# Spreading gate tiles over a recurrence: four tiles per three chunks instead of four per four

## The chip, the cores and the metric

The kernel runs on one core of a Trainium2 chip. The metric is the device time of one execution in microseconds (us), median of several. A fast run has a granted TensorE clock of 0.97 to 0.99 over the whole run. Ratios are the mean time of one kernel's fast runs over that of the kernel before in the same rounds on the same chip, so they are not quite the ratio of the medians quoted beside them. The studies ran on several chips; the kernel before has a median of 509.9 us on the first and 508.4 to 508.6 us, with a spread of 506.6 to 510.8, on the others.

## The reference

```python
# q, k, v, alpha: (4, 8, 768, 48)
for t in range(S):                      # gated linear attention
    state = alpha[:, :, t, :, None] * state + einsum('bhd,bhe->bhde', k[:, :, t], v[:, :, t])
    y[:, :, t] = einsum('bhd,bhde->bhe', q[:, :, t], state)
x = y as (3072 tokens, 384)
out = ((x @ w1) * (x @ w2)) @ w3 @ w_out      # w1, w2: 384x1024; w3: 1024x1024; w_out: 1024x384
```

The recurrence is computed in chunks of 128 tokens, 24 in all (six per batch row). Every three chunks give a group of 384 tokens; a group's gate product `(x@w1)*(x@w2)` is made in eight tiles of 128 columns. `w3 @ w_out` is folded once and multiplied last. The weights come as 64-bit floats and are converted on the chip.

## The kernel before

TensorE is shared by two kinds of work: attention, chunk after chunk, and gate tiles. A gate tile is a generator with two *pieces* of nine matmuls each; `run(k)` issues k pieces from a queue, at three places in a chunk.

```python
def split_x(g, i):                  # x of a group becomes three exact parts
    x = st.pop(("xT", g))
    t = tr[i].tile([C, 3, KM, TG], FP32R, tag="x3", name="x3")    # one buffer
    nc.scalar.activation(t[:, 0], x, AF.Copy, scale=1.0 - 2.0 ** -13)           # L369
    nc.vector.tensor_sub(t[:, 1], x, t[:, 0].bitcast(FP32))                     # L370
    nc.vector.scalar_tensor_tensor(t[:, 2], ...)                                # L371

def exact(to, w, x, scale):         # one piece
    # six matmuls with parts 0 and 1 (L380), evacuation on ScalarE (L382),
    # three matmuls with part 2 (L384), sum on VectorE (L385)
    ...
def gate(g, f):                     # one tile: exact(...); yield; exact(...); product (L396), store

FH = CW // C                        # 4
begin = {4 + 4 * g: (g, range(FH if g < 4 else KF)) for g in range(5)}
for n in range(N):
    ...                             # loads ahead
    scores(n)                       # L326, then masks on VectorE (L329)
    if n - 1 in begin:
        g, tiles = begin[n - 1]
        split_x(g, 0)
        fill.extend(gate(g, f) for f in tiles)
    ...
    convert(1, 2 if n == 0 else 3)  # weight conversion steps
    run(n - 1 not in begin)         # first place
    advance(n)
    outer(n)                        # L298; not in the last chunk of a batch row
    ...
    transposed(n + 1)               # L287, copies L288
    decayed(n + 2)                  # VectorE, L268
    ...
    if n in begin:
        load_x(begin[n][0], nc.scalar)
    ...
    run(1)                          # middle place
    decays(n + 3)                   # L256
    ...
    attend(n)                       # L345, L348, copies L352
    run(n - 1 in begin)             # last place
```

A chunk with a split uses the middle and the last place, any other chunk the first and the middle one. Since there is a single buffer of split x, `split_x` must wait until the previous group's last matmul has read the old parts. After the loop, a second part works off the remaining tiles (`todo`), two buffers of split x in turn, with the folding of `w3 @ w_out` among them, and then projects.

Of the kernel before, what the change touches and what calls it, by code (L numbers as in the profile page):

```python
# [48 lines left out]
def kernel(  # L49
# [22 lines left out]
    KF = DF // C  # L72
    G = 3
    NG = N // G
# [46 lines left out]
    def load_a(n):  # L121
        if n < N:
            st["a", n] = inp.tile([C, H, D], FP32, tag="ac", name="ac")
            nc.sync.dma_start(out=st["a", n], in_=rows(alpha, n))

    def load_kq(n):
        if n >= N:
            return
        st["kq", n] = inp.tile([C, 2, H, D], FP32, tag="kq", name="kq")
        nc.sync.dma_start(out=st["kq", n][:, 0], in_=rows(k, n))  # L130
        nc.sync.dma_start(out=st["kq", n][:, 1], in_=rows(q, n))

    def load_v(n):
        if n < N:
            st["v", n] = vs[n % len(vs)]
            nc.sync.dma_start(out=st["v", n][:, :, 0:D], in_=rows(v, n))
# [77 lines left out]
    def convert(steps, ahead=3):  # L214

        for _ in range(steps):
            while weights and len(begun) < ahead:
                begun.append(weights.popleft())
                next(begun[-1])
            if not begun:  # L220
                return
            x = begun.popleft()
            try:
                next(x)
                begun.appendleft(x)
            except StopIteration:
                pass
# [5 lines left out]
    def logs(n):  # L233
        if n >= N:
            return
        a = st.pop(("a", n)).rearrange("p h d -> p (h d)")
        la = st["la", n] = work.tile([C, DM], FP32, tag="la", name="la")
        nc.scalar.activation(la, a, AF.Ln)
        if n >= LATE:

            t = st["la", n] = work.tile([C, 2, DM], FP32R, tag="la2", name="la2", bufs=1)
            nc.scalar.copy(t[:, 0], la)
            nc.vector.tensor_sub(t[:, 1], la, t[:, 0].bitcast(FP32))
        if n in ends:
            nc.scalar.dma_start(out=ends[n][2:3], in_=a[0:1])

    def decays(n):
        if n >= N:
            return
        lc = bank()[:, 0:DM]  # L250
        la = st.pop(("la", n))
        if n < LATE:
            nc.tensor.matmul(lc, utri if n % 2 else after, la, start=True, stop=True)
        else:
            for i in range(2):
                nc.tensor.matmul(lc, sums[:, n % 2], la[:, i], start=(i == 0), stop=(i == 1))  # L256

        e = st["e", n] = work.tile([C, 2, DM], FP32, tag="e", name="e", bufs=3)
        nc.scalar.activation(e[:, 0], lc, AF.Exp, scale=-1.0)
        nc.scalar.activation(e[:, 1], lc, AF.Exp)  # L260
        if n in ends:
            nc.scalar.dma_start(out=ends[n][0:1], in_=e[0:1, 0])
        if n + 1 in ends:
            nc.scalar.dma_start(out=ends[n + 1][1:2], in_=e[C - 1:C, 1])
# [26 lines left out]
    def outer(n):  # L291
        if n >= N or last(n):
            return
        qk, vc = qks[n % 3], st["v", n]
        s1 = bank()[:, 0:NP * D].rearrange("p (j d) -> p j d", j=NP)
        for j in range(NP):
            for i in range(2):
                nc.tensor.matmul(s1[ds(DP * i, DP), j, :], qk[:, 0, 2 * j + i, :], vc[:, 2 * j + i, 0:D],  # L298
                                 start=True, stop=True)

        if n % 2:
            to = st["T", n] = work.tile([C, NP, D], FP32, tag="tmp", name="tmp")
        else:
            to = Ts[1][:, :, 0:D]
        if n % NCH == 0:
            nc.vector.tensor_copy(out=to, in_=s1)
        else:
            nc.vector.tensor_add(to, s1, Ts[n % 2][:, :, 0:D])

    def advance(n):  # L310

        if n not in ends:
            return
        dec, d = work.tile([C, NP], FP32, tag="dec", name="dec"), decs[n // 2 % 2]
        nc.gpsimd.tensor_mul(dec, d[:, 0, :], d[:, 1, :])
        nc.gpsimd.tensor_mul(dec, dec, d[:, 2, :])
        nc.gpsimd.tensor_tensor(Ts[0][:, :, 0:D], st.pop(("T", n - 1)),
                                dec[:, :, None].to_broadcast([C, NP, D]), op=ALU.mult)

    def scores(n):  # L320
        qkT = st["qkT", n]
        sc = [bank().rearrange("p (j c) -> p j c", j=NP) for _ in range(2)]
        for j in range(NP):
            for i in range(2):
                r = ds(DP * i, D)
                nc.tensor.matmul(sc[i][:, j, :], qkT[r, 0, j, :], qkT[r, 1, j, :], start=True, stop=True)  # L326
        ms = work.tile([C, 2, NP, C], FP32, tag="ms", name="ms")
        for i in range(2):
            nc.vector.tensor_tensor(ms[:, i].bitcast(I32), sc[i].bitcast(I32), keep_bc, op=ALU.bitwise_and)  # L329
        st["ms", n] = ms  # L330
# [34 lines left out]
    def split_x(g, i):  # L365
        x = st.pop(("xT", g))
        t = tr[i].tile([C, 3, KM, TG], FP32R, tag="x3", name="x3")
        st["x3", g] = t
        nc.scalar.activation(t[:, 0], x, AF.Copy, scale=1.0 - 2.0 ** -13)  # L369
        nc.vector.tensor_sub(t[:, 1], x, t[:, 0].bitcast(FP32))  # L370
        nc.vector.scalar_tensor_tensor(t[:, 2], t[:, 0].bitcast(FP32), 1.0 + 1.0 / P, x,  # L371
                                       op0=ALU.mult, op1=ALU.subtract)
# [14 lines left out]
    def gate(g, f):  # L387
        r = []
        x = [[st["x3", g][:, part, kk, :] for kk in range(KM)] for part in range(3)]
        for i, scale in enumerate((1.0, P * P)):  # L390
            r.append(gw.tile([C, TG], FP32, tag="r", name="r"))
            exact(r[-1], [[w12[:, part, i, kk, ds(f * C, C)] for kk in range(KM)] for part in range(3)], x, scale)
            if len(r) == 1:
                yield
        ab = abp.tile([C, TG], FP32, tag="ab", name="ab")
        nc.vector.tensor_mul(ab, *r)  # L396
        store_ab()
        st["ab"] = g, f, ab
# [62 lines left out]
    def run(pieces):  # L461

        for _ in range(pieces):
            if not fill:
                return
            try:
                next(fill[0])
            except StopIteration:
                fill.popleft()

    FH = CW // C
# [16 lines left out]
    load_kq(3)  # L488
    load_a(4)

    begin = {4 + 4 * g: (g, range(FH if g < 4 else KF)) for g in range(5)}
    for n in range(N):
        load_v(n + AHEAD - 1)
        load_a(n + 5)
        load_kq(n + AHEAD)
        scores(n)
# [4 lines that stand above are left out]
        if n == 0:  # L501
            logs(2)
            decays(2)
            logs(3)
        early = n < 7
        convert(1, 2 if n == 0 else 3)
        run(n - 1 not in begin)
        advance(n)
        outer(n)
        if early:  # L510
            convert(1)
        transposed(n + 1)
        decayed(n + 2)
        logs(n + 4)
        if n in begin:
            load_x(begin[n][0], nc.scalar)
        convert(early and n > 2)
        run(1)
        decays(n + 3)
        load_ends(n + 2)  # L520
        convert(early or n % 3 == 0)
        attend(n)
        run(n - 1 in begin)
    part1.close()


# [6 lines left out]
    folds, folded = deque(), 0  # L533
# [4 lines left out]
            weights.append(load_w3(i, c0))  # L538

    todo, order = list(fill), []  # L540
    visits = [(g, range(FH, KF)) for g in range(4)] + [(g, range(KF)) for g in range(len(begin), NG)]
    for k, (g, tiles) in enumerate(visits):
        order.append((max(len(todo) - 4, order[-1][0] + 1 if order else 0), len(todo), g, 1 - k % 2))
        todo += [gate(g, f) for f in tiles]
    owed = 0.0
    load_x(order[0][2])
    lastp = None
    for i, x in enumerate(todo):
        while order and i >= order[0][0]:
            split_x(*order.pop(0)[2:])  # L550
            if order:
                load_x(order[0][2])
        for _ in x:
            pass
        owed += 2.7 if folds or folded else 1.2
        convert(int(owed))
        owed -= int(owed)
        if folded < KF:
            if folds and next(folds[0], None) is None:
                folds.popleft()  # L560
                folded += 1
        elif lastp is None:
            folding.close()
            conversion.close()
            lastp = pool("lastp", 1, reuse_waits="tile")
            for n in range(4):
                load_ab(n)
# [37 lines left out]
```

## Time and profile before

| | before |
|---|---|
| median | 509.87 us (509.72 to 509.97, 4 runs) |
| span of the profiled run | 506.3 us |
| attention's last store is issued | 214.3 us |
| from there to the end | 292.0 us |
| TensorE gaps from 0.25 us, after 60 us, before attention ends | 4.8 us |

The store of a chunk's output (`xd<-x`) follows its attention products at once, so its 24 issue times serve as a clock of the chunks. A gap is the bracket behind a line of TensorE's timeline: idle time before the line, and what ended it. The prediction shows the page and the gaps.

### The profile page before, as it was taken

To read this page: it belongs to the slowest core of one execution; us is meant where nothing else is said; L and a number is where in the kernel's file an instruction comes from. 1 tells how busy PE (TensorE), PEld (TensorE's weight loads), DVE (VectorE), ACT (ScalarE), POOL (GpSimd) and SP (SyncE) were. 2 spreads that over 40 slices of the span, in tenths; PEclk is the share of its full clock that TensorE was granted. 3 is DMA by queue.
4 is the path that set the end of the run, shared out by engine and by line. 5 is a ranking of instruction groups with operands and counts; after the bars stand their busy time and mean duration, and the time that the engine had idled before them with its cause. 6 is when DMAs were issued, how large, how long until landed. Compare 5 with 4: busy or idle time off the path is not lost.

```text
span 506.3 us, 9496 instructions
## 1 busy us (share of the span) xinstructions
PE 476.6 (94%) x3568; PEld 426.5 (84%) x3568; DVE 371.6 (73%) x620; ACT 250.7 (50%) x479; POOL 16.2 (3%) x43
## 2 busy tenths in 40 slices
PE   3878499999799999999999999999999999999997
PEld 2666388887688888899999988898889899999996
DVE  2777797999777667599999987877434597777771
ACT  3664664867487544365555545454223433333330
POOL 2000002200110000000000000000000000000000
PEclk9979699999899999999999999999999999999999
DMA  9989999999976733165665443321100776655511
GB/s 173 181 216 228 216 215 241 222 225 231 227 173 161 159 80 105 56 178 174 193 193 173 171 159 102 126 88 49 46 33 31 197 231 185 178 174 176 178 54 47
DMA packets 168734, 79.08 MB, mean 156 GB/s; under 512 B 112856, under 2 KB 162544, under 8 KB 168688
## 3 DMA queue, kind: packets, MB, share of 16 engines
q1 hardware_dynamic: 147184, 70.73, 55.3%
q10 hardware_dynamic: 21504, 7.75, 6.7%
q8 instruction: 28, 0.46, 0.4%
q14 instruction: 18, 0.15, 0.1%
HBM read 56.40 MB, written 22.06 MB: 155 GB/s over the span
## 4 chain that ended last, share of the span: by engine, by line
PE 73%; DVE 1%; issue 0%; DVEq 0%
PE bank L380 37%; PE bank L384 18%; PE bank L429 8%; PE bank L348 2%; PE bank L326 2%; PE bank L287 2%; PE bank L423 1%; PE bank L345 1%; PE bank L298 1%; PE bank L256 1%; DVE x L371 0%; DVE x L370 0%; DVE o L385 0%; DVEq L385 0%
## 5 line engine op out<-in xcount | busy, mean ns | idle before, releaser
L380 PE MATMUL bank<-x,w 128*128 128x384 f32 x768 | 162.8, 346 | 10.3 <-ACT x L369 8.0
L380 PEld LDWEIGHTS bank<-x,w 128*128 128x128 f32 x768 | 133.4, 189 | 16.6 <-ACT x L369 8.4
L382 ACT ACTIVATE t<-bank 128x384 f32<-128x384 f32 x152 | 74.4, 491 | 131.8 <-PE bank L380 103.0
L385 DVE SCALAR_TENSOR_TENSOR r<-bank,t 128x384 f32<-128x384 f32 x128 | 69.6, 554 | 49.6 <-ACT t L382 38.3
L384 PE MATMUL bank<-x,w 128*128 128x384 f32 x384 | 88.3, 337 | 1.3 <-DVE x L371 1.3
L384 PEld LDWEIGHTS bank<-x,w 128*128 128x128 f32 x384 | 68.6, 189 | 2.6 <-PE bank L380 1.4
L380 PE MATMUL bank<-w3o,ab 128*128 128x384 f32 x384 | 70.4, 334 | 0.0
L380 PEld LDWEIGHTS bank<-w3o,ab 128*128 128x128 f32 x384 | 66.9, 188 | 0.0
L429 PE MATMUL bank<-wo,w3T 128*128 128x384 f32 x128 | 42.6, 486 | 0.0
L384 PE MATMUL bank<-w3o,ab 128*128 128x384 f32 x192 | 37.2, 334 | 0.0
L429 PEld LDWEIGHTS bank<-wo,w3T 128*128 128x128 f32 x128 | 24.2, 189 | 14.9
L189 ACT ACTIVATE rest<-raw 128x512 f32<-128x512 uint32 (+1 forms) x36 | 23.3, 650 | 26.1 <-DMA raw<-in_moe_w_dram 23.6
L396 DVE TENSOR_TENSOR ab<-r 128x384 f32<-128x384 f32 x64 | 35.5, 555 | 0.9
L448 DVE TENSOR_TENSOR ab<-abl,ab 128x1024 fp32r<-128x1024 f32 x24 | 29.4, 1224 | 9.1 <-ACT ab L447 9.1
L447 ACT ACTIVATE ab<-abl 128x1024 fp32r<-128x1024 f32 x24 | 25.5, 1062 | 19.9 <-PE bank L384 18.8
L384 PEld LDWEIGHTS bank<-w3o,ab 128*128 128x128 f32 x192 | 33.6, 188 | 0.0
L329 DVE TENSOR_TENSOR ms<-bank,keep 128x512 int32<-128x512 int32 x48 | 31.1, 683 | 2.4 <-PE bank L326 2.4
L326 PE MATMUL bank<-qkT 48*128 48x128 f32 x384 | 28.8, 291 | 4.1 <-ACT qkT L288 4.1
L326 PEld LDWEIGHTS bank<-qkT 48*128 48x128 f32 x384 | 24.1, 193 | 9.6 <-ACT qkT L288 5.9
L287 PE MATMUL bank<-ident,qk 128*128 128x128 f32 x192 | 27.9, 291 | 3.9 <-DVE qk L268 3.9
L288 ACT COPY qkT<-bank 128x512 f32<-128x512 f32 x48 | 25.7, 586 | 10.2 <-PE bank L287 8.8
L268 DVE TENSOR_TENSOR qk<-kq,e 128x768 f32<-128x768 f32 x24 | 22.9, 954 | 10.2 <-ACT e L260 5.7
(65 smaller groups left out, 516.6 us busy)
## 6 DMA issues: line engine op xcount, KB each, us to landing
abd<-ab SPq DMA_DIRECT2D x64, 192.0 KB, 2.6
abl<-abd SPq DMA_DIRECT2D x24, 512.0 KB, 4.5
raw<-in_moe_w_dram SPq DMA_DIRECT2D x16, 512.0 KB, 4.4
raw<-in_moe_w_dram SPq DMA_DIRECT2D x24, 256.0 KB, 4.7
ac<-in_alpha_dram SPq DMA_DIRECT2D x24, 192.0 KB, 5.5
kq<-in_k_dram SPq DMA_DIRECT2D x24, 192.0 KB, 5.1
kq<-in_q_dram SPq DMA_DIRECT2D x24, 192.0 KB, 4.9
v<-in_v_dram SPq DMA_DIRECT2D x24, 192.0 KB, 4.7
```

Of the source, the lines that this page charges most:

```text
L287: nc.tensor.transpose(tp[:, ds(j * C, C)], qk[:, i, 2 * j:2 * j + 2, :], ident)
L288: nc.scalar.copy(qkT[:, i], tp.rearrange("p (j c) -> p j c", j=NP))
L326: nc.tensor.matmul(sc[i][:, j, :], qkT[r, 0, j, :], qkT[r, 1, j, :], start=True, stop=True)
L329: nc.vector.tensor_tensor(ms[:, i].bitcast(I32), sc[i].bitcast(I32), keep_bc, op=ALU.bitwise_and)
L380: nc.tensor.matmul(p1, w[part][i], x[part][i], start=(part == i == 0), stop=(part == 1 and i == n - 1))
L382: nc.scalar.activation(t, p1, AF.Copy, scale=(1.0 + 1.0 / P) * scale)
L384: nc.tensor.matmul(p2, w[2][i], x[2][i], start=(i == 0), stop=(i == n - 1))
L385: nc.vector.scalar_tensor_tensor(to, p2, -scale, t, op0=ALU.mult, op1=ALU.add)
L396: nc.vector.tensor_mul(ab, *r)
L429: nc.tensor.matmul(po, w3T[:, j, :], wo[:, j, :], start=(j == 0), stop=(j == KF - 1))
L447: nc.scalar.activation(t[:, 0], ab, AF.Copy, scale=1.0 - 2.0 ** -13)
L448: nc.vector.tensor_sub(t[:, 1], ab, t[:, 0].bitcast(FP32))
```

## The change

It starts a gate group every three chunks early on, puts a third piece into chunks 6, 7, 9, 10, 12 and 13 (at the last place), and so brings three more tiles (22 in place of 19) into the attention part, where TensorE shows gaps. The conversion rates are raised so that folding keeps its distance from the end of a shorter `todo`.

```diff
-    begin = {4 + 4 * g: (g, range(FH if g < 4 else KF)) for g in range(5)}
+    begin = {at: (g, range(FH)) for g, at in enumerate((4, 7, 10, 13, 17, 21))}
...
-        run(n - 1 in begin)
+        run(n - 1 in begin or 4 < n < 14)
...
-    visits = [(g, range(FH, KF)) for g in range(4)] + [(g, range(KF)) for g in range(len(begin), NG)]
+    visits = [(g, range(FH, KF)) for g in range(len(begin))] + [(g, range(KF)) for g in range(len(begin), NG)]
...
-        owed += 2.7 if folds or folded else 1.2
+        owed += 2.8 if folds or folded else 1.3
```

## The prediction

The marked cuts took out statements that no trace or run of this case shows. The sum comes to -2.0 us as printed and was put at -2.6. "That of 126.31 us" is the split of x in chunk 13 of the kernel before.

> **What bounds the kernel now.** I read the page first: busy totals and the 40 slices.
>
> ```profile
> PE 476.6 (94%) x3568; PEld 426.5 (84%) x3568; DVE 371.6 (73%) x620; ACT 250.7 (50%) x479; POOL 16.2 (3%) x43
> ...
> PE   3878499999799999999999999999999999999997
> ...
> PEclk9979699999899999999999999999999999999999
> DMA  9989999999976733165665443321100776655511
> ```
>
> TensorE is the bound, but its row is full of nines even where DMA is full too, in the first 11 slices (to about 140 us). Only the start and slice 5 (50 to 63 us) lie clearly below nine. So I cut the run into stages at the starts of gate groups, read from when the splits of x ran (55, 90, 126, 159, 190 us, then every 12.5 us).
>
> ```profile
> core 0: us, PE busy (x) PEld busy (x) DVE busy (x) ACT busy (x) POOL busy (x), PEclk, DMA share, GB/s
> 55.00:82.00 27.00, 24.82 (x222) 19.85 (x222) 24.72 (x46) 17.96 (x38) 2.76 (x3) 0.84 1.11 235
> 82.00:110.00 28.00, 27.27 (x302) 23.53 (x301) 24.52 (x43) 18.19 (x41) 2.56 (x3) 1.00 1.14 225
> 110.00:137.00 27.00, 22.86 (x222) 18.73 (x220) 23.63 (x42) 17.24 (x39) 2.84 (x3) 0.94 1.01 225
> ...
> 160.00:191.00 31.00, 31.00 (x348) 27.19 (x342) 20.43 (x34) 17.66 (x40) 1.30 (x5) 1.00 0.53 116
> ...
> 250.00:295.00 45.00, 45.00 (x262) 44.96 (x261) 43.08 (x79) 25.16 (x45) 0.00 (x0) 1.00 0.57 190
> ```
>
> From 55 to 137 us (chunks 5 to 13) DMA is saturated, VectorE is at about 90% and TensorE has slack. From 137 us TensorE sets the pace at full clock, and from 214 us it does nothing but gates, folds and projection, back to back. Where the slack is, TensorE's timeline shows, keeping the gaps from 0.5 us:
>
> ```profile
> 56.32 1.33 PE L380 MATMUL bank<-x,w 128*128 128x384 f32 x3 [6.27 <-ACT x L369]
> 58.48 1.33 PE L380 MATMUL bank<-x,w 128*128 128x384 f32 x3 [0.83 <-DVE x L370]
> ...
> 94.67 0.76 PE L384 MATMUL bank<-x,w 128*128 128x384 f32 x3 [0.73 <-DVE x L371]
> ...
> 127.53 0.79 PE L380 MATMUL bank<-x,w 128*128 128x384 f32 x3 [1.70 <-ACT x L369]
> 129.83 0.79 PE L380 MATMUL bank<-x,w 128*128 128x384 f32 x3 [1.51 <-DVE x L370]
> 131.19 0.87 PE L384 MATMUL bank<-x,w 128*128 128x384 f32 x3 [0.57 <-DVE x L371]
> ```
>
> Every one stands at the start of a gate group: TensorE waits until x of the new group has been split in three. There is one buffer of split x in this part, so the split follows the last gate of the old group. At 160 and 191 us, with DMA and VectorE calmer, the same boundary shows no gap.
>
> To size the slack I take start-to-start spacings from the same timeline: gate matmul 0.171 us (146 in 25 us), score 0.068, transpose 0.103, outer product and state product 0.037, value product 0.064, log sum 0.22 (0.32 in the older form). Times the counts between 55 and 137 us (162, 128, 64, 112 and 112, 144, 14 and 4) this is 27.8 + 8.7 + 6.6 + 8.3 + 9.2 + 4.4 = 65 us of work in 82 us: 17 us of slack. The same sum for 160 to 191 us is 30 of 31. Of the 17 us, about 7 are the gaps above (counting from 55 us), about 5 are granted clock below one, and some 5 are small waits that the modelled busy time covers.
>
> [...] PE reads 31 of 31 and 45 of 45, yet PEld is 88% and 100%; in 110 to 137 us it is 69%. [...] after the gap of 6.27 us the granted clock is 0.50 from 55 to 60 us and 0.66 in the next five; after the three gaps near 130 us, 0.67 from 130 to 135. [...] that of 126.31 us starts behind two evacuations of attention output, and its VectorE halves start at 128.44 and 129.70, among masks, copies and weight conversions. [...] the windows to 137 us show a share over 1 at only 225 to 235 GB/s.
>
> **The change, part by part.** A gate tile is two pieces of nine matmuls. Before, from chunk 5 on, each chunk carries two pieces: 38, so 19 tiles in the attention part; 45 visits remain. After, groups begin at 4, 7, 10, 13, 17, 21, each with four tiles, and chunks 6, 7, 9, 10, 12 and 13 carry three pieces (at 5, 8 and 11 the split takes one away): 24 pieces in chunks 5 to 13 against 18, and 20 against 20 in chunks 14 to 23. That is 22 tiles in the first part and 42 visits after. The 64 tiles are the same ones; three have moved.
>
> 1. Removed from the second part: 3 tiles of 18 matmuls at 0.171, or 3.1 us each (12.48 us per four between splits): **-9.3 us**, all on TensorE's path there.
> 2. Added to chunks 5 to 13: the same three. Mixed with attention a piece takes longer: six matmuls 1.15 us and three 0.52 to 0.6, so about 3.35 us per tile: **+10 us of TensorE work**, into 17 us of slack.
> 3. Slack lost and won there. Old boundaries: chunk 9 (0.7 us), chunk 13 (3.8 us of gaps and about 1.6 us of lost clock, 0.06 x 27). Sum about 6, which goes. New boundaries: chunks 8, 11, 14. Ideally a split is 1.17 + 1.27 + 1.27 = 3.7 us before the third part can be used, against 1.16 + 0.67 + 1.09 = 2.9 us of scores, outer products and transposes, so a bare boundary costs near 1 us and a crowded one 3 or 4. I choose 1.7 us: 5 in all. The first one, near 56 us, is untouched: the third piece comes only later, and the wait hangs on loads before it. Of the small waits I let the added work between dependent steps win back 2 to 3 us. Net: **-3.5 us**.
> 4. Two more splits (12 to 14 in all): 1.17 us of ScalarE and 2.5 us of VectorE each. In the second part four tiles per split becomes the rule for 24 tiles in place of 16, and conversion goes from 1.2 to 1.3 steps a tile. VectorE's start-to-start costs are 0.47 per gate operation, 2.54 per split, 1.95 per three steps of the output weight and 2.48 of w3: 1.41 + 0.64 + 1.3 x 0.65 to 0.83 = 2.9 to 3.1 us per tile. That equals TensorE's 3.1, so nearly hidden: **+0.3 us**.
> 5. The hand-over at the end of attention: before, the first new split has four or five unfinished tiles ahead of it; now two, 6.2 us. Before, attention's last matmuls end near 213.7 us, that split starts at 217.49 and ends at 221.7, 8 us later; its third part is needed 6.2 + 1.0 = 7.2 us later. **+0.5 us**, between 0 and 2.
> 6. Folding: counting the conversion steps through the loop, the last fold ends at visit 42 of 45 before and 39 of 42 after, two visits from the end both times; the faster rates only keep that margin. **0**.
>
> Sum: -9.3 + 10 - 3.5 + 0.3 + 0.5 = -2.0; the slack might pay for more, since the 5 us of small waits are the least known, so I put **-2.6 us: 507.2 us**.
>
> **Rivals.** (a) The added tiles are free: chunks 5 to 13 are paced by loads and VectorE, and TensorE has 17 us of slack for 10. Then the whole 9.3 us is won: 500.5. For it: DMA share over 1. Against it: after 60 us compute waits for loads are few (about 2.0, 1.4 and 0.9 us)[...]. (b) DMA or VectorE take over: per chunk comes a third of a tile's store more (192 KB a tile) and a 576 KB reload of x every three chunks instead of four. That is 1.2 MB more in the stage, at 230 GB/s an estimated 5 us, in which case the stage lengthens by 5 us and about 4 us are won: 505.5. VectorE gets 3 x 1.41 + 2.54 = 6.8 us more. (c) Boundaries multiply the wait: three crowded ones like that at 127 us, each 5 us with its cold clock, against 6 us before: 9 us lost on top of 10 added for 9.3 moved, tempered by small waits: 515.
>
> **Range and chances.** Even with all slack after 60 us used the gain is about 10 us, just 2% (10.2 us), so faster is unlikely: 0.05. Slower by 2% needs rival (c) in full and more: 0.03. Within: 0.92. Range 501.5 to 511.5: (a) nearly whole on one side, half of (c) on the other.
>
> **What would show it.** Gate products before the last attention copy should be 22 in place of 19. The stretch from the first split to the one at chunk 14 should last some 88 to 90 us against 82 to the end of chunk 13; from there to the end of attention about as before; from there to the end of the run 9 us less. Gaps after the splits of chunks 8, 11 and 14 below 2 us with clock 1.00 support step 3; gaps of 3 us or a clock near 0.7 support (c). If DMA waits appear in front of logs or decayed queries, (b). A gap at the first or third gate group after attention would be step 5; a gap where projection begins would refute step 6.

## The result, and the profile after

| | before | after |
|---|---|---|
| median | 509.87 us | 516.98 us (515.12 to 518.10, 4 runs) |
| ratio | | 1.0136, 95% interval 1.0103 to 1.0169 |
| span of the profiled run | 506.3 | 516.1 |
| last attention store | 214.3 | 232.7 |
| from there to the end | 292.0 | 283.4 |
| gaps after 60 us, before attention ends | 4.8 | 9.4 |

The changed kernel is slower by 1.4%, outside the predicted range. By the 2% that a verdict asks for this is still "the same", to which the prediction gave 0.92, but the sign is the opposite one. The page of the changed kernel:

```profile
PE 482.4 (93%) x3568; PEld 429.1 (83%) x3568; DVE 376.2 (73%) x624; ACT 253.5 (49%) x481; POOL 13.6 (3%) x43
...
PE   3877698996998999999999999999999999999997
...
PEclk9979699998799999999999999999999999999999
DMA  9999999986777555135646555432001576565611
```

TensorE's row has new dents in slices 7, 10 and 13, and the clock row an 8 and a 7 in slices 10 and 11 (116 to 142 us), where it had a 9 and an 8. DMA is *less* full than before in slices 9 to 11 (8, 6 and 7, before 9, 9 and 9): transfers don't hold this stretch up. The second part first; windows from the last attention store to the end, of before and of after:

```profile
214.30:506.30 292.00, 288.38 (x1577) 270.79 (x1575) 214.77 (x347) 125.25 (x210) 0.00 (x0) 1.00 0.44 137
```

```profile
232.70:516.10 283.40, 279.45 (x1523) 261.44 (x1521) 211.69 (x340) 122.80 (x205) 0.00 (x0) 1.00 0.45 141
```

The first number after the window is its length, the next is TensorE's busy time with its instructions. 54 matmuls fewer, three tiles of 18, and 8.6 us less: this part does what was intended. The loss is all in the attention part, which ends 18.5 us later. Windows there (after):

```profile
core 0: us, PE busy (x) PEld busy (x) DVE busy (x) ACT busy (x) POOL busy (x), PEclk, DMA share, GB/s
...
118.30:131.90 13.60, 8.91 (x61) 6.66 (x58) 12.69 (x23) 6.56 (x15) 0.00 (x0) 0.74 0.51 122
```

In 118 to 132 us TensorE does 61 matmuls in 13.6 us at a clock of 0.74, while VectorE is busy 12.69 of 13.60. The gaps of TensorE at the starts of the groups (after; the split at chunk 5, near 56 us, is as before and left out):

```profile
90.21 0.79 PE L380 MATMUL bank<-x,w 128*128 128x384 f32 x3 [1.68 <-DVE x L370]
91.48 0.80 PE L384 MATMUL bank<-x,w 128*128 128x384 f32 x3 [0.48 <-DVE x L371]
...
120.78 0.80 PE L380 MATMUL bank<-x,w 128*128 128x384 f32 x3 [1.07 <-ACT x L369]
125.17 1.33 PE L380 MATMUL bank<-x,w 128*128 128x384 f32 x3 [3.59 <-DVE x L370]
...
158.08 0.80 PE L380 MATMUL bank<-x,w 128*128 128x384 f32 x3 [0.96 <-DVE x L370]
159.35 0.80 PE L384 MATMUL bank<-x,w 128*128 128x384 f32 x3 [0.47 <-DVE x L371]
```

These are chunks 8, 11 and 14. Each waits for the split; the middle one, 4.66 us together, is the worst. What the clock makes of it, in windows of 2 us (the number before the last two is the granted clock):

```profile
124.00:126.00 2.00, 0.83 (x3) 0.82 (x3) 2.00 (x2) 0.00 (x0) 0.00 (x0) 0.73 0.30 109
126.00:128.00 2.00, 1.97 (x7) 1.46 (x5) 1.66 (x4) 0.49 (x1) 0.00 (x0) 0.50 0.03 8
...
132.00:134.00 2.00, 2.00 (x8) 2.00 (x7) 0.53 (x2) 0.59 (x2) 0.00 (x0) 0.50 0.72 158
134.00:136.00 2.00, 2.00 (x19) 1.44 (x18) 0.56 (x1) 0.80 (x2) 0.00 (x0) 0.71 1.28 247
```

All four windows from 126 to 134 us are at 0.50, so 0.27 x 2 + 0.50 x 8 + 0.29 x 2 = 5.1 us of clock are lost behind this one boundary. Before, the worst boundary (chunk 13) had 3.78 us of gaps, and the same sum over its windows of 0.92, 0.50 and 0.72 gives 1.7 us.

The 18.5 us of the attention part come together about like this. Added work: the prediction's 10 us (the second experiment below measures 10.7). Gaps: 9.4 less 4.8 is 4.6 us. Clock after 60 us: summed over windows of 2 us in the same way, 6.9 us are lost after and 3.4 before, so 3.4 us more (3.42 unrounded). Sum 18.0. The account is rough: for experiment 5 below the same three terms give 10.9 us, and its attention ends only 8.0 us later than before.

Why is chunk 11 so bad? TensorE just ahead of the gap (after):

```profile
116.92 0.69 PE L384 MATMUL bank<-x,w 128*128 128x384 f32 x3
117.53 1.16 PE L326 MATMUL bank<-qkT 48*128 48x128 f32 x16
118.62 1.09 PE L287 MATMUL bank<-ident,qk 128*128 128x128 f32 x8
```

The L384 at 116.92 is the old group's last: the third piece of chunk 10, at the *last* place of the chunk, behind the attention products. The split can start only then. Until the new group's first piece (120.78, in the list of gaps above), TensorE has scores and transposes, 2.2 us; outer products, 0.6 us elsewhere, are missing because chunk 11 ends a batch row. And VectorE's queue, in the same kernel:

```profile
118.36 0.69 DVE L209 SCALAR_TENSOR_TENSOR w<-w,mant 128x512 fp32r<-128x512 f32 x1
...
121.64 0.55 DVE L385 SCALAR_TENSOR_TENSOR r<-bank,t 128x384 f32<-128x384 f32 x1
122.10 0.68 DVE L329 TENSOR_TENSOR ms<-bank,keep 128x512 int32<-128x512 int32 x1
122.70 0.55 DVE L396 TENSOR_TENSOR ab<-r 128x384 f32<-128x384 f32 x1
123.17 0.68 DVE L329 TENSOR_TENSOR ms<-bank,keep 128x512 int32<-128x512 int32 x1
123.77 1.34 DVE L370 TENSOR_TENSOR x<-xT,x 128x1152 fp32r<-128x1152 f32 x1
125.03 1.35 DVE L371 SCALAR_TENSOR_TENSOR x<-x,xT 128x1152 fp32r<-128x1152 f32 x1
```

ScalarE's half of the split was finished at 120.7 us (119.57 plus 1.16), yet VectorE comes to L370 only at 123.77. From 118.36 to 121.64 it does six weight-conversion steps (L209 is the first), and then the last piece's own evacuation and product and the new chunk's masks. It isn't idle in between. So the late piece takes away the cover, and conversions are part of what makes the queue ahead of the split long.

### The profile page after: what moved, and what is told of

The parts are those of the page before. It is cut to its first block, busy times and chain, and to the rows that moved or that the text cites. A ratio compares the mean times of both kernels' runs of the same rounds, so it can differ in the third digit from the quotient of the medians.

```text
span 516.1 us, 9499 instructions
## 1 busy us (share of the span) xinstructions
PE 482.4 (93%) x3568; PEld 429.1 (83%) x3568; DVE 376.2 (73%) x624; ACT 253.5 (49%) x481; POOL 13.6 (3%) x43
## 4 chain that ended last, share of the span: by engine, by line
PE 67%; DVE 2%; issue 0%; DVEq 0%
PE bank L380 33%; PE bank L384 17%; PE bank L429 8%; PE bank L348 2%; PE bank L326 2%; PE bank L287 2%; PE bank L423 1%; PE bank L345 1%; PE bank L298 1%; DVE x L371 1%; PE bank L256 0%; DVE wo L199 0%; DVE x L370 0%; DVE r L385 0%; DVE o L385 0%
## 5 line engine op out<-in xcount | busy, mean ns | idle before, releaser
L380 PE MATMUL bank<-x,w 128*128 128x384 f32 x768 | 165.6, 350 | 15.0 <-ACT x L369 7.2
L384 PE MATMUL bank<-x,w 128*128 128x384 f32 x384 | 89.4, 341 | 1.5 <-DVE x L371 1.4
L384 PEld LDWEIGHTS bank<-x,w 128*128 128x128 f32 x384 | 69.4, 191 | 3.4 <-DVE x L371 2.4
L384 PE MATMUL bank<-w3o,ab 128*128 128x384 f32 x192 | 37.1, 334 | 0.0
L384 PEld LDWEIGHTS bank<-w3o,ab 128*128 128x128 f32 x192 | 33.6, 188 | 0.0
L268 DVE TENSOR_TENSOR qk<-kq,e 128x768 f32<-128x768 f32 x24 | 22.9, 955 | 10.8 <-ACT e L260 6.2
```

What stands on the lines that cost most here:

```text
L380: nc.tensor.matmul(p1, w[part][i], x[part][i], start=(part == i == 0), stop=(part == 1 and i == n - 1))
L384: nc.tensor.matmul(p2, w[2][i], x[2][i], start=(i == 0), stop=(i == n - 1))
```

## The experiments

Theories at the start: **B**, the more frequent boundaries cost; **F**, slack of TensorE can't be filled, so that the added tiles cost their time and more; **C**, splits queue behind weight conversions. After the first four runs came **D**, the *place* of the last piece, against **P**, three pieces per chunk are too many wherever they stand.

**1. The groups alone.** The kernel before, old conversion rates included, with the groups of the changed kernel: three tiles per three chunks, no third piece.

```diff
+    begin = {at: (g, range(3 if g < 3 else FH)) for g, at in enumerate((4, 7, 10, 13, 17, 21))}
+        run(n - 1 in begin)
+    visits = [(g, range(3 if g < 3 else FH, KF)) for g in range(len(begin))] + ...
```

> Groups at chunks 4, 7, 10, 13, 17, 21 as in the changed kernel, but three tiles over three chunks and no third piece: nine tiles in chunks 5 to 13, as before the change. Only the earlier and more frequent splits are left of the change. Theory B (the group boundaries cost, with the clock lost behind them): attention ends 7 to 9 us later than before (near 222 us), the rest is as long as before, total 516 to 519. Theory F (slack of TensorE in chunks 5 to 13 cannot be filled, so the added tiles cost all of it): attention ends at most 2 us later, total 509 to 512.

Measured: 507.5 us, ratio 0.9997 (0.9956 to 1.0039). Attention's last store stands at 211.4 us, 2.9 us *earlier* than before. Theory B falls in this form: boundaries at chunks 8, 11 and 14 cost nothing by being there. (F's interval for this run, 509 to 512 us, was missed too: the earlier groups are a small gain.) Their gaps here are 1.1, 1.6 and 0 us, and the clock after 60 us reads 1.00. From there to the end it takes 292.7 us against 292.0: two more splits in all, 0.7 us.

**2. The tiles alone.** Kernel before with its boundaries, a fifth tile (a repeat, so the result is right) in groups 0 to 2 and a third piece at the last place in six chunks that are not a group's last.

```diff
+    begin = {4 + 4 * g: (g, [*range(FH), 0] if g < 3 else range(FH if g < 4 else KF)) for g in range(5)}
+        run(n - 1 in begin or n in (6, 7, 10, 11, 14, 15))
```

> Groups at chunks 4, 8, 12, 16, 20 as before the change, but the first three groups carry a fifth tile (a repeat of tile 0, so the result stays right) and chunks 6, 7, 10, 11, 14, 15 a third piece: three more tiles at the old boundaries, and three more in all. The part after attention is as long as before. Theory B: part of the added 10 us falls into slack, attention ends 5 to 9 us later (219 to 223 us), total 515 to 519. Theory F: nothing is absorbed and queues get longer, attention ends 12 to 18 us later, total 522 to 528.

Measured: 519.12 us, ratio 1.0213 (1.0180 to 1.0246); attention's last store at 224.9 us, 10.7 us later, the rest 291.9 us. It lies between the theories' intervals for that time: three tiles cost what they take, 10 us and a little; nothing of the slack is filled, nothing beyond is lost. Only four of the six pieces stand in chunks 5 to 13, where the prediction saw slack. But there it is the same: from the scores of chunk 5 to those of chunk 14 it takes 97.4 us against 89.3, 8.1 us more for the 6.7 us of two tiles. With the first experiment: -2.9 for the groups and +10.7 for the tiles, 8 us, where the change as a whole costs 18.5. The rest comes only from the two together.

**3 and 4. Half the conversion.** Before and after, without loading and converting the second half of w1 and w2 (set to one; wrong result).

```diff
-    for c0 in range(0, DF, CW // 2):
+    for c0 in range(0, CW, CW // 2):
...
+    nc.gpsimd.memset(w12[:, :, :, :, CW:].bitcast(FP32), 1.0)
```

> The kernel before, without loading and converting the second half of w1 and w2 (set to one; the result is wrong on purpose). It takes 3.1 MB of loads and some 20 us of VectorE and 12 us of ScalarE out of the attention part. It serves as the base for the next run. If conversions crowd the boundaries (theory C), the gaps near 91 and 127 us shrink below 1 us each and attention ends 6 to 12 us earlier. If not, it ends less than 4 us earlier.

> The changed kernel without the second half of w1 and w2 (wrong result on purpose), to be read against the previous run. Theory C (the change loses because splits queue behind weight conversions on VectorE and ScalarE): here it no longer loses, total within 1 us of the previous run or below it by up to 6. Theories B without crowding, or F: it stays 5 to 9 us slower than the previous run.

Measured: 500.68 us (attention's last store at 207.5) and 512.66 us (231.0). The kernel before does what theory C expected of it: after 60 us one gap of 0.83 us is left of 4.8, and attention ends 6.8 us earlier, so conversions do lengthen its boundaries. But C expected the changed kernel to come within 1 us of that, and the distance between the two kernels, 12 us, is larger than with the full conversion (7 us; 8.7 on this chip, by experiment 8). So the loss isn't explained by these conversions. In the second run the gap has moved to chunk 8 (1.27 and 3.30 us), where the output weight's conversion has come forward into the freed place; conversion at the boundary was thus thinned out but not removed, and the run doesn't say what a boundary without any would cost.

**5 and 6. The third piece elsewhere in the chunk.** Same pieces per chunk and same groups as the changed kernel.

```diff
-        run(n - 1 not in begin)
+        run((n - 1 not in begin) * (1 + (4 < n < 14)))            # 5: at the first place
...
-        run(1)
+        run(1 + (n - 1 not in begin and 4 < n < 14))              # 6: at the middle place
...
-        run(n - 1 in begin or 4 < n < 14)
+        run(n - 1 in begin)                                       # 5 and 6
```

> The changed kernel, with the third piece of a chunk moved from the end of the chunk (behind the attention products, directly before the next chunk's scores and, every third time, the split) to its first place. Theory D (the change loses because the last piece of a group now stands directly before the split that has to wait for it, so neither the attention products nor their evacuation cover the split): gaps behind the splits of chunks 8, 11 and 14 fall below 1 us each, the clock stays near 1.00 there, attention ends near 223 to 226 us instead of 233, total 507 to 511. Theory P (three pieces per chunk are too much for this stretch wherever they stand): attention ends at 231 us or later, total 515 to 518.

> The same with the third piece at the second place, before the decays and the attention products: the last piece of a group ends where it does in the kernel before. Theory D: total 507 to 511, as the run before this one. Theory P: 515 to 518.

Measured: 508.42 us, ratio 1.0006 (0.9968 to 1.0044), and 508.14 us, ratio 0.9998 (0.9961 to 1.0035). Theory P falls, D holds in the time: the whole loss goes with the place of one piece. The detail of D was wrong at chunk 8, which still has a gap of 3.58 us (2.75 in the other run) and loses 3.4 us of clock behind it: there, more cover did not help. ScalarE's half was done at 86.6 us, and VectorE came to L370 only at 90.01, so its queue set the wait. But chunk 11 shows what has changed (run 5, TensorE):

```profile
115.99 0.68 PE L384 MATMUL bank<-x,w 128*128 128x384 f32 x3
116.51 0.50 PE L256 MATMUL bank<-la,sums 128*128 128x384 f32 x2
116.94 0.67 PE L345 MATMUL bank<-qkT,T 48*64 48x128 f32 x16
117.54 1.09 PE L348 MATMUL bank<-ms,v 128*64 128x128 f32 x16
118.56 1.16 PE L326 MATMUL bank<-qkT 48*128 48x128 f32 x16
119.66 1.09 PE L287 MATMUL bank<-ident,qk 128*128 128x128 f32 x8
120.50 1.29 PE L380 MATMUL bank<-x,w 128*128 128x384 f32 x6
122.26 0.76 PE L384 MATMUL bank<-x,w 128*128 128x384 f32 x3 [0.46 <-DVE x L371]
```

Between the old group's last matmul (115.99) and the new group's first (120.50) lie log sums, attention products, scores and transposes: 4.0 us from 116.5 on, against 2.2 us with the late piece. The split runs beneath them and only 0.46 us is left; the clock stays at 1.00 from 110 to 124 us.

**7. The same defect put into the kernel before.** The second piece of every chunk without a split goes to the last place; nothing else changes.

```diff
-        run(1)
+        run(n - 1 in begin)
...
-        run(n - 1 in begin)
+        run(1)
```

> The kernel before the change, same tiles and groups, only that the second piece of a chunk without a split is moved from before the decays to the end of the chunk. Theory D: the gaps at the splits of chunks 9, 13, 17 and 21 grow by 1 to 3 us each and attention ends 4 to 9 us later, total 513 to 518. Theory P: no change, 508 to 511.

Measured: 519.96 us, ratio 1.0239 (1.0191 to 1.0286), more than D expected; attention's last store 13 us later, gaps at chunks 9, 13, 17 and 21 of 6.3, 2.4, 2.2 and 1.1 us (in the profiled run, at 523.07 us the slowest of the four). At chunk 13 alone the gap is smaller than before (3.8 us). With old groups, old tiles and old rates, the place alone costs 11 us.

**8. The changed kernel again**, as yardstick on the same chip.

> The changed kernel once more, on the same chip as the three above, as their yardstick: 515 to 518 by all theories, attention ends at 231 to 234 us.

Measured: 517.31 us, ratio 1.0175 (1.0142 to 1.0209), the last attention store at 232.5 us, with the same gaps at chunk 11 (1.06 and 3.60 us). The clock lost behind them is 3.4 us here, not 5.1, and chunk 8 has 3.4 us of gaps and 1.7 us of clock: how the loss is shared out among the boundaries varies between profiles.

**9 and 10. Which late pieces?** Late only in chunks 7, 10, 13, the last of a group; then only in 6, 9, 12.

```diff
+        run((n - 1 not in begin) * (1 + (n in (6, 9, 12))))       # 9; in 10: (7, 10, 13)
...
+        run(n - 1 in begin or n in (7, 10, 13))                   # 9; in 10: (6, 9, 12)
```

> The changed kernel with the third piece at the end of the chunk only in chunks 7, 10 and 13, the last of a group; in chunks 6, 9 and 12 it stands first. Theory D1 (only the group's last piece, directly before the split, costs): total 515 to 518, attention ends 230 to 234 us. Theory D2 (a piece between a chunk's attention products and the next scores costs in any chunk): about half of the loss, 511 to 513.5.

> The reverse: late in chunks 6, 9 and 12, first in 7, 10 and 13. Theory D1: 506.5 to 510, attention ends 221 to 224 us, like the run with all third pieces first. Theory D2: 511 to 513.5.

Measured: 517.66 us, ratio 1.0178 (1.0149 to 1.0208), and 509.09 us, ratio 1.0014 (0.9979 to 1.0048). All of the loss belongs to the three pieces that stand directly before a split; the other three cost nothing in that place that the runs can tell from zero (attention's last store is at 225.1 us, 1 us later than D1 expected).

**11 and 12. Cover added.** Third pieces first, and in the chunk with the split both new pieces only after the attention products; then the same postponement in the kernel before.

```diff
-        run(1)
+        run(n - 1 not in begin)
...
+        run(2 * (n - 1 in begin))
```

> All third pieces first, and in the chunk with the split both pieces of the new group only after the attention products, so that scores, outer products, transposes, decays and attention products, some 4.5 us, lie between split and first use. Theory D1 (cover of the split is what counts): gaps at chunks 8, 11, 14 nearly gone, also the 3.6 us at chunk 8 that the run with the third piece first still had; total 502 to 506, faster than both kernels. If cover no longer counts: 507 to 509.

> The same in the kernel before: in chunks 5, 9, 13, 17, 21 both pieces after the attention products. Theory D1: the 3.8 us of gaps at chunk 13 and the clock lost behind them go, total 503 to 507. If cover doesn't count: 508 to 510.

Measured: 507.1 us, ratio 0.9962 (0.9927 to 0.9996), and 507.05 us, ratio 0.9985 (0.9935 to 1.0034). The waits for the split become small, as expected, but only 1 to 2 us is won, and the first total lies in the interval for "cover no longer counts". Other waits appear, of TensorE for masks (2.10 us near 118 us in run 11; 1.67 near 113 in run 12) and for evacuations, and they take the clock too: in each of the two runs 5.1 us of clock are lost after 60 us (granted clock 0.97 from there to attention's last store), against 3.4 in the kernel before (0.98). In run 11 cover moves the queue's delay to the next things that wait for VectorE (2.10 us for masks, 2.20 us near 97 us for an evacuation); in run 12 an evacuation on ScalarE is waited for as well (2.29 us near 111 us). The edit also covers the first split, in chunk 5, which brings 4 to 5 us of its own (from the scores of chunk 5 to those of chunk 6 it takes 14.2 and 13.2 us, against 18.4 before).

**13. The late pieces kept, cover added.** This is the decisive one: the changed kernel exactly, only the first piece of each new group is postponed, at all six splits.

```diff
-        run(1)
+        run(n - 1 not in begin)
...
-        run(n - 1 in begin or 4 < n < 14)
+        run(2 if n - 1 in begin else 4 < n < 14)
```

> The changed kernel with the late third pieces as they are, and only the first piece of a new group postponed behind the attention products of its first chunk, as the run with covered splits did. Missing cover as the cause: the gaps and the lost clock at chunks 8, 11 and 14 go, total 507 to 511. If the late piece costs in another way (it delays scores or occupies queues): 514 to 518.

Measured: 506.34 us (503.84 to 507.89), ratio 0.9950 (0.9896 to 1.0004). The late pieces are where they were, and the loss is gone. Chunk 11 in this run, TensorE:

```profile
114.01 1.09 PE L287 MATMUL bank<-ident,qk 128*128 128x128 f32 x8
114.86 0.60 PE L256 MATMUL bank<-la,sums 128*128 128x384 f32 x2
115.39 0.67 PE L345 MATMUL bank<-qkT,T 48*64 48x128 f32 x16
118.30 0.65 PE L348 MATMUL bank<-ms,v 128*64 128x128 f32 x6 [2.24 <-DVE ms L329]
119.36 0.88 PE L348 MATMUL bank<-ms,v 128*64 128x128 f32 x10 [0.41 <-DVE ms L329]
120.17 2.11 PE L380 MATMUL bank<-x,w 128*128 128x384 f32 x6
```

The new group starts at 120.17 without a wait. VectorE's order is the old one (mask, product, mask, then L370 at 119.22), and TensorE now waits 2.65 us for the masks, in place of 4.66 us for the split. The clock dips for less long:

```profile
120.00:122.00 2.00, 2.00 (x10) 1.65 (x7) 2.00 (x3) 1.18 (x3) 0.00 (x0) 0.60 0.62 184
122.00:124.00 2.00, 2.00 (x8) 2.00 (x8) 2.00 (x4) 0.49 (x1) 0.00 (x0) 0.55 0.76 158
```

It is 1.00 after, so 1.7 us are lost in place of 5.1 (3.4 in run 8). Attention's last store is at 221.6 us, 11.1 us earlier than in the changed kernel. Over the stretch after 60 us, gaps fall from 9.4 to 5.3 us and the lost clock from 6.9 to 1.7 us: 9.2 of the 11.1.

Not all of this undoes the change. The time from the start of a chunk's scores to the start of the next chunk's, read from TensorE's timelines, tells where it is won:

| us | before | changed | again (8) | pieces first (5) | late but covered (13) |
|---|---|---|---|---|---|
| chunk 5 | 18.4 | 18.5 | 18.1 | 19.2 | 14.3 |
| chunk 8 | 8.1 | 10.8 | 13.7 | 14.8 | 9.8 |
| chunk 11 | 7.3 | 17.0 | 15.7 | 8.2 | 12.2 |
| chunk 14 | 8.0 | 10.0 | 10.0 | 8.0 | 8.1 |

(Before, chunks 8, 11 and 14 have no split; the splits in chunks 9 and 13 give 9.1 and 14.1.) Cover gives back 7.8 us in chunks 8, 11 and 14; another 4.2 come from chunk 5, whose wait the change had not touched. So cover explains most of the loss, not every microsecond of it.

**14. The late pieces kept, the split written ahead of the scores.**

```diff
+        if n - 1 in begin: ... split_x(g, 0) ...
         scores(n)
-        if n - 1 in begin: ... split_x(g, 0) ...
```

> The changed kernel with the split written ahead of the new chunk's scores. Its VectorE half then stands at most one mask earlier in the queue. Queue order as the cause: one to two thirds of the loss goes, total 510 to 514. Missing cover as the cause: 514.5 to 518.

Measured: 515.79 us, ratio 1.0138 (1.0099 to 1.0176). Little changes; gaps at chunk 11 are 1.28 and 3.21 us. That fits missing cover. As a test of queue order it is weak: in the built program the split moved ahead of one mask at chunks 8 and 14, and at chunk 11 of none.

Whether a second buffer of split x removes the wait for the old group's last reader was not shown. It could not be tried: with two buffers the build of the changed kernel stops, with the message that the attention part's pool of work tiles needs 36.6 KB per partition where 27.2 KB are left.

## Why the prediction was wrong, point by point

- **Step 1 with 4, 5 and 6 (the second part): right.** -9.3, +0.3, +0.5 and 0 make -8.5 us; the part shrank by 8.6. The hand-over cost a gap of 0.47 us at 240.2 us, and projection begins without one.
- **Step 2 (the added work): right.** +10 was predicted; experiment 2 measured 10.7 for three tiles in that stretch.
- **Step 3 failed.** It read "Net: **-3.5 us**"; measured is 18.5 less 10, that is +8.5 us, 4.6 of it gaps and 3.4 clock. Its term of boundaries, "a bare boundary costs near 1 us and a crowded one 3 or 4. I choose 1.7 us: 5 in all", gave old and new boundaries the same cover behind the split: scores, outer products, transposes. It never asked where in the chunk the old group *ends*. The added third piece stands behind the attention products, so the old group's last matmul moved from before them to after them, and 2 us of cover went. Gaps of 1.1, 1.6 and 0 us at the three boundaries without third pieces (experiment 1), and of 3.6, 0.5 and 0 with the pieces first (experiment 5), show that 5 us in all was no bad figure for covered ones; uncovered they took 2.2, 4.7 and 1.4 us, plus 5.1 us of clock behind the middle one. The "2 to 3 us" that added work should win back from small waits are not shown: in experiment 2 nothing was absorbed, while the account of experiment 5 leaves 2.9 us that nothing explains.
- **The rivals.** (c) named the right kind of event (gaps behind splits, cold clock behind them) and 515 us, and I put it at the edge: its premise was three equally crowded boundaries. In the profiled run it took only one with a long clock loss, in run 8 two shorter ones. (a) is refuted by experiment 2. (b) is refuted by the windows: DMA fell to 122 GB/s where the time was lost. VectorE is part of it: it is busy 12.69 of 13.60 us there, and its queue sets how long this split takes once started (119.57 to 126.38 us; VectorE's two parts begin at 123.77 and 125.03). But it was just as full with the pieces first (14.00 of 14.00 us from 110 to 124 us in run 5), without the loss.
- **The range.** Its upper end assumed half of (c). The signs to watch for were the right ones: the prediction said that gaps of 3 us or a clock near 0.7 at chunks 8, 11 and 14 would support (c), and 3.59 us and 0.74 is what came. From the first split to that of chunk 14 it took 99.5 us (54.43 to 153.92) against the forecast 88 to 90.
- **A reading.** "Only the start and slice 5 lie clearly below nine" overlooks the 7 in slice 11 of the row (127 to 139 us), the crowded boundary of chunk 13; its gaps are in the prediction all the same.

What stays open: how much of a boundary's length is weight conversion, since experiment 4 didn't empty the queue of it; why chunk 8 was no shorter with the pieces first; what sets how long the clock stays low (in the changed kernel it read 0.50 in the windows from 126 to 134 us, although TensorE's timeline shows no gap there; in the kernel before it read 0.50 from 132 to 134 us, behind gaps of 1.70, 1.51 and 0.57 us with six matmuls between them, and 1.00 again from 136 us); and whether the 0.4 to 0.5% that experiments 11 and 13 show over the kernel before is real, as one interval ends at 0.9996 and the other at 1.0004. If it is, it need not be the change's: the kernel before with the same cover (experiment 12) measured 507.05 us. The change brings no clear gain in any form: it moves 9 us of work from a full stretch into one that absorbs none of it.

## What to carry to other kernels

Where one buffer is refilled between two groups of work, what the refill cost here was its length, with whatever was queued ahead of it, less the work that stood between the old group's last reader and the new group's first reader (at chunk 11, 2.2 us of such work left 4.66 us of gaps, and 4.0 us left 0.46); before adding work, look at where in the program order that last reader ends up. Repair it by giving the engine something independent at that very place: here postponing one piece per group was worth 11 us, 4 of them at a split that had waited all along. And idle time on the bounding engine wasn't room by itself here: three added tiles came on top (10.7 us for some 10 us of work, experiment 2), and a boundary with 4.66 us of gaps took 5.1 us of clock with it in one profile and 3.4 in another.
